# Two of seven normalised tiles transposed by VectorE blocks and on-chip DMAs instead of TensorE

## The chip, the cores and the metric

One core of a Trainium2 chip runs the whole kernel. The metric is the time on the device in microseconds, the median of a few runs; one execution is also recorded by the hardware profiler, and all rows below come from that one. PE is TensorE (PEld its weight loads), DVE is VectorE, ACT is ScalarE, POOL is GpSimd, and SP is the engine that issues the DMAs here.

## The reference: what is computed

Attention over 2 batches and 12 heads (448 positions, 64 dimensions each, scores capped by a tanh), whose output is laid out as 896 tokens of 768 values. Then two feed-forward blocks:

```
h = x @ w_in                                   # 896 x 1024
solu = h * softmax(h)
ln = (solu - mean) / sqrt(var + 1e-6) * g_ln   # per token
x2 = ln @ w_out                                # 896 x 768
out = (silu(x2 @ w_gate) * (x2 @ w_val)) @ w_out2
```

All numbers stay near float32: each operand is kept as a rounded part `hi` and a remainder `lo`, and a product is three matmuls (hi·hi, hi·lo, lo·hi).

## The kernel before, in words

The change lies in the first feed-forward block. The 896 tokens are seven tiles of 128 (t = 0 to 6). For each tile, `ff1_h(t)` computes h on PE in six steps of six matmuls of 512 columns into two PSUM banks, and its `tail` does the softmax and the norm: DVE takes the two maxima (TENSOR_REDUCE) and negates them, ACT takes the exponentials of both halves, DVE sums, takes the reciprocal, multiplies (two SCALAR_TENSOR_TENSOR) and gathers the variance (BN_STATS, BN_AGGR), POOL takes the power -1/2, and DVE (ACT from tile 4 on) applies scale and shift to 128x1024 values in the tile `ee`. Tiles 5 and 6 take their variance by squares on ACT. The small numbers live in `sms`.

`ff1_T(t)` then transposes the normed tile for the next product. PE does eight transposes of 128x128 in two PSUM banks `lt` (two runs of four), ACT copies each bank to the hi part (`hi_act`), DVE subtracts to get the lo part (`lo_dve`). Tiles 0 to 2 land in `lA` (384 columns), tiles 3 to 6 in `lB` (512).

`load_w_out(j)` brings a block of 128 columns of w_out in two halves (i = 0, 1; contraction chunks 0 to 3 and 4 to 7), in the order j = 0, 3, 1, 4, 2, 5. Each half goes through SP's load into one of two raw buffers, one ACT pass (`wo<-wo_raw`; two for j = 4, 2, 5), up to four DVE passes that end with the fill of the low bits from the raw buffer, four ACT passes of 128 columns that multiply by g_ln (`wo<-wo,gt`), the hi copy on ACT (`wo<-wo`, output rounded) and the lo subtraction on DVE. The blocks use three buffers of the pool `wo`. `ff1_x2(j, ...)` is the product of such a block with `lA` or `lB`; it is cut after the fourth chunk, so the second half of a product needs the second half of the block.

What PE does is a fixed list, each step written out in `run` (T[t] are the transposes of tile t, wo[i] the i-th block's loading, x2[i] its products):

```
steps = h[1] + h[2][:1] + T[0] + h[2][1:] + h[3][:1] + T[1] + h[3][1:] + wo[0] + h[4][:2] + T[2] + ...
steps = x2[0][0] + x2[0][1] + wo[2] + x2[1][0][:1] + T5 + x2[1][0][1:] + x2[1][1] + T6
steps += wo[3] + x2[2][0][:1] + x2[0][2] + x2[1][2] + ...
```

PE keeps this order; for DVE, ACT and SP a scheduler sets the order when the program is built (an instruction recorded while `in_order` is true keeps its place in the program). On the chip each engine works through its fixed queue in order, and an instruction whose operand is late holds all behind it on that engine. All calls go through one helper, so most rows carry line L54, and one goes by the tile names.

Of the kernel before, what the change touches and what calls it, by code (L numbers as in the profile page):

```python
# [5 lines left out]
F32 = mybir.dt.float32  # L6
# [55 lines left out]
class Kernel:  # L62
# [507 lines left out]
    def ff1_T(self, t, get, o):  # L570

        nc = self.nc

        def go(g):
            def f():
                l = get()
                ps = self.pt.tile([128, 512], F32, name=f"lt_{t}_{g}", tag=self.ttag)
                for i in range(4):
                    fc = 4 * g + i
                    self.transpose(ps[:, i * 128:(i + 1) * 128], self.ln[t][:, fc * 128:(fc + 1) * 128], self.ident)  # L580
                pv = ps.rearrange("p (i n) -> p i n", i=4)
                hi, lo = (l[:, 4 * g:4 * g + 4, u, o:o + 128] for u in range(2))
                self.hi_act(hi, pv)
                self.lo_dve(lo, pv, hi)
            return f

        return [(0.45, go(g)) for g in range(self.K1 // 4)]

    def load_w_out(self, j):

        w = self.wos[j] = self.wo.tile([128, 2, self.K1, 128], F32R, name=f"wo_{j}", tag="wo")
        for i in range(2):
            c = slice(4 * i, 4 * i + 4)
            src = self.w_out[i * 512:(i + 1) * 512, j * 128:(j + 1) * 128].rearrange("(f p) d -> p f d", p=128)
            if j in (4, 2, 5):
                f = self.f32_shifted(self.load_shifted(src, f"wo_{j}_{i}"), f"wo_{j}_{i}")
            else:
                f = self.f32(self.load64(src, f"wo_{j}_{i}"), f"wo_{j}_{i}", pin=True)
            f = f.rearrange("p (f d) -> p f d", f=4)
            for m in range(4):  # L600
                self.A.activation(f[:, m], f[:, m], AF.Copy, scale=self.gt[:, 4 * i + m:4 * i + m + 1])
            self.hi_act(w[:, 0, c], f)
            self.lo_dve(w[:, 1, c], f, w[:, 0, c])
# [92 lines left out]
    def x_hi(self, i):  # L696

        self.hi_act(self.T[i][:, 0], self.xf[i])

    def x_lo(self, i):  # L700

        self.lo_dve(self.T[i][:, 1], self.xf[i], self.T[i][:, 0])

# [138 lines left out]
    def seven_products(self, fc):  # L842
# [11 lines left out]
        X = lambda kh, th: [[self.x2[3 * kh + c][:, u, 448 * th:448 * th + 448] for u in range(2)] for c in range(3)]  # L854
        T1, T2, T3, T4 = ([[t[:, u, c] for u in range(2)] for c in range(3)] for t in self.T)

# [78 lines left out]
    def split(self, d, src):  # L935

        self.hi_act(d[0], src)
        self.lo_dve(d[1], src, d[0])
# [226 lines left out]
    def run(self):  # L1165
        nc = self.nc
        KD, K1, K2, F1 = self.KD, self.K1, self.K2, self.F1
# [17 lines left out]
        f, g, hi, lo = zip(*w)  # L1185
        self.w_steps = [((), f[0][:1], ()), (f[0][1:2], (), f[0][2:] + g[0][:1]), ((), (g[0][1], hi[0]), (lo[0],))]
        for i in range(1, KD):
            a = g[i][:1]
# [9 lines left out]
        h = [self.ff1_h(t) for t in range(7)]  # L1198
# [9 lines left out]
        st = self.pool("st", side="right")  # L1208
# [5 lines left out]
        self.pt = self.ph = self.pool("pm", bufs=8, space=PSUM)  # L1214
        self.htag, self.ttag = "m", "m"
        lA = self.slot("l", [128, K1, 2, 384], "lA")
        T = [self.ff1_T(t, lambda: lA, 128 * t) for t in range(3)]
        lp = self.pool("lp", side="right")
        self.wo = self.pool("wo", bufs=3, side="right")
        lB = lp.tile([128, K1, 2, 512], F32R, name="lB", tag="lB")  # L1220
        T3, T4 = self.ff1_T(3, lambda: lB, 0), self.ff1_T(4, lambda: lB, 128)
        T5, T6 = self.ff1_T(5, lambda: lB, 256), self.ff1_T(6, lambda: lB, 384)
        J = (0, 3, 1, 4, 2, 5)
        wo = [[(0.0, lambda j=j: self.load_w_out(j))] for j in J]
# [2 lines left out]
        whole = (blocks[0], (lambda: lB, 512, 384))  # L1227
        x2 = [[self.ff1_x2(j, *b) for b in (blocks if i < 2 else whole)] for i, j in enumerate(J)]

        steps = h[1] + h[2][:1] + T[0] + h[2][1:] + h[3][:1] + T[1] + h[3][1:] + wo[0] + h[4][:2] + T[2] + h[4][2:] + wo[1] + h[5][:5] + T3 + h[5][5:] + h[6][:-1] + T4 + h[6][-1:]  # L1230
        for _, f in steps:
            f()
        wp.release()
        n = self.HN = self.DM // 2
# [9 lines left out]
        steps = x2[0][0] + x2[0][1] + wo[2] + x2[1][0][:1] + T5 + x2[1][0][1:] + x2[1][1] + T6  # L1244
        steps += wo[3] + x2[2][0][:1] + x2[0][2] + x2[1][2] + [(0.0, lambda j=j: self.x_sums0(j)) for j in J[:2]]
        for j in range(2, KD):
# [4 lines left out]
            a, b = x2[j]  # L1251
# [10 lines left out]
        a12 = ap.tile([128, KD * 2 * 896], F32R, name="a_1", tag="a_1")  # L1262
        self.T = [a12[:, 2688 * i:2688 * i + 2688].rearrange("p (u k n) -> p u k n", u=2, k=3) for i in range(4)]
        self.A12t, self.A22t = (a12[:, KD * 2 * a:KD * 2 * z].rearrange("p (k u n) -> p k u n", k=KD, u=2)
# [89 lines left out]
```

## Time and profile before

| | |
|---|---|
| median of 3 runs | 471.57 us (470.81 to 471.76) |
| profiled execution, its own time | 471.51 us |
| its span, first to last instruction | 469.8 us |
| PE busy | 465.2 us, 99% of the span |
| DVE busy, ACT busy | 382.4 us (81%), 315.3 us (67%) |
| SP's DMA queue | 65936 packets, 51.84 MB |

The share of PE says that the time is the length of PE's list plus whatever PE has to wait; 1.7 us lie outside of the span. The first feed-forward block takes from about 108 to 228 us.

### The profile page before, as it was taken

Reading aid. Unit: us, or ns where it says so; the run is one execution under the profiler, and the core shown is the slowest. Engines: PE = TensorE matmul, PEld = TensorE weight load, DVE = VectorE, ACT = ScalarE, POOL = GpSimd, SP = SyncE. Lnnn points to the kernel's source line nnn. Section 1 sums busy time; section 2 is a strip of 40 time slices with the busy share of each in tenths; the row PEclk is TensorE's granted clock in tenths of the full one; section 3 lists DMA queues with packets and bytes.
Section 4 is the critical chain, followed back from the end, with each engine's and each line's share of the span. In section 5 each row is a group of like instructions: output and inputs, shape, how many; then the busy total and the mean of one; then the engine's idle time right before and its main releaser. Section 6 shows DMA issues by size and latency. Waiting matters only on the chain.

```text
span 469.8 us, 7726 instructions
## 1 busy us (share of the span) xinstructions
PE 465.2 (99%) x2970; PEld 385.1 (82%) x2970; DVE 382.4 (81%) x671; ACT 315.3 (67%) x480; POOL 37.2 (8%) x76
## 2 busy tenths in 40 slices
PE   9999999999999999999999999999999999999997
PEld 8444444446888899998989999999998889999996
DVE  3689999987777997766698989988897777999961
ACT  4999999961223699889676667766589988525200
POOL 1011010112000000000003211011000000000000
PEclk9999999999999999999999999999999999999999
DMA  7985575002000233535215523323447774010021
GB/s 179 215 201 117 165 190 165 21 1 77 14 1 0 78 102 116 175 114 178 91 46 184 173 87 130 120 76 124 136 134 221 249 207 130 26 43 18 0 85 67
DMA packets 66004, 52.33 MB, mean 111 GB/s; under 512 B 35760, under 2 KB 62128, under 8 KB 65200
## 3 DMA queue, kind: packets, MB, share of 16 engines
q1 hardware_dynamic: 65936, 51.84, 37.4%
q8 instruction: 23, 0.38, 0.3%
q14 instruction: 13, 0.11, 0.1%
q0 software_dynamic: 32, 0.00, 0.0%
HBM read 49.08 MB, written 2.75 MB: 110 GB/s over the span
## 4 chain that ended last, share of the span: by engine, by line
PE 99%; DVE 1%; issue 0%
PE p L54 17%; PE x L54 13%; PE g L54 12%; PE h L54 12%; PE pv L54 8%; PE sc L54 7%; PE b L54 6%; PE v L54 6%; PE c L54 6%; PE S L54 4%; PE e L54 3%; PE lt L54 1%; PE T L54 1%; PE warm L54 1%; DVE ks L54 0%; PE d L54 0%
## 5 line engine op out<-in xcount | busy, mean ns | idle before, releaser
L54 PE MATMUL g<-x,g 128*128 128x448 f32 (+2 forms) x288 | 62.2, 364 | 0.0
L54 PE MATMUL h<-wi,x 128*128 128x512 f32 x252 | 59.1, 392 | 0.0
L54 PEld LDWEIGHTS g<-x,g 128*128 128x128 f32 x288 | 53.2, 188 | 5.2
L54 PEld LDWEIGHTS h<-wi,x 128*128 128x128 f32 x252 | 46.8, 188 | 11.2 <-issue 1.5
L54 ACT ACTIVATE P<-sc,consts 112x896 f32<-112x896 f32 x48 | 45.4, 1010 | 3.8 <-PE sc L54 2.2
L54 ACT ACTIVATE P<-P,consts 112x3584 f32<-112x3584 f32 (+1 forms) x13 | 39.7, 3061 | 0.1
L54 PE MATMUL pv<-P,v 112*32 112x448 f32 x384 | 38.5, 540 | 0.0
L54 PEld LDWEIGHTS sc<-ks 64*112 64x112 f32 x288 | 23.3, 171 | 18.3 <-issue 8.4
L54 PE MATMUL sc<-ks 64*112 64x448 f32 x288 | 35.9, 379 | 0.2
L54 PE MATMUL x<-lB,wo 128*128 128x256 f32 (+1 forms) x192 | 35.2, 337 | 0.0
L54 PEld LDWEIGHTS x<-lB,wo 128*128 128x128 f32 x192 | 29.6, 189 | 3.4
L54 PE MATMUL b<-a,g 128*128 128x448 f32 x144 | 31.8, 365 | 0.0
L54 ACT ACTIVATE ee<-h,sms 128x512 f32<-128x512 f32 x14 | 9.5, 684 | 33.2 <-DVE sms L54 33.2
L54 PEld LDWEIGHTS pv<-P,v 112*32 112x32 f32 x384 | 12.2, 110 | 23.0 <-issue 20.9
L54 PE MATMUL v<-x,g 128*128 128x384 f32 (+1 forms) x144 | 30.1, 362 | 0.0
L54 PEld LDWEIGHTS b<-a,g 128*128 128x128 f32 x144 | 27.1, 188 | 2.1
L54 PEld LDWEIGHTS v<-x,g 128*128 128x128 f32 x144 | 26.1, 188 | 2.8
L54 PE MATMUL x<-lA,wo 128*128 128x384 f32 x144 | 27.2, 338 | 0.0
L54 PEld LDWEIGHTS x<-lA,wo 128*128 128x128 f32 x144 | 25.2, 188 | 0.5
L54 PE MATMUL S<-P,ones 112*32 112x448 f32 x192 | 22.4, 549 | 0.0
L54 POOL COPY sm<-tr 32x14 f32<-32x14 f32 x48 | 15.0, 312 | 93.0 <-DVE tr L54 91.5
L54 DVE TENSOR_TENSOR x<-x,x 128x448 fp32r<-128x448 f32 (+3 forms) x26 | 15.3, 588 | 8.3 <-ACT x L54 7.6
(277 smaller groups left out, 970.4 us busy)
## 6 DMA issues: line engine op xcount, KB each, us to landing
wg_raw<-in_moe_w_gate_dram SPq DMA_DIRECT2D x11, 765.8 KB, 4.2
wv_raw<-in_moe_w_val_dram SPq DMA_DIRECT2D x10, 765.8 KB, 4.3
h<-in_moe_w_out_dram SPq DMA_DIRECT2D x18, 383.6 KB, 3.6
wi_raw<-in_moe_w_in_dram SPq DMA_DIRECT2D x6, 1024.0 KB, 6.3
wo_raw<-in_moe_w_out_dram SPq DMA_DIRECT2D x6, 512.0 KB, 3.5
wo_raw<-in_moe_w_out_dram SPq DMA_DIRECT2D x6, 510.5 KB, 3.7
v<-in_v_dram SPq DMA_DIRECT2D x24, 112.0 KB, 3.4
kq<-in_k_dram SPq DMA_DIRECT2D x22, 112.0 KB, 3.1
```

The costliest lines, as they stand in the source:

```text
L54: i = f(*a, **k)
```

## The change

For tiles 0 and 1, the PE transposes with their PSUM banks, four ACT copies and four DVE subtractions go. In their place `moved` takes a buffer of the pool `wo`, transposes the normed tile on DVE in blocks of 32x32 (one STREAM_TRANSPOSE of 128x1024 into the first half `y`), and puts the blocks where a full transpose has them by 16 DMAs per tile (`y` to `z`, each 32 partitions by 8 by 32 values). `split` then makes hi and lo of all 128x1024 values at once, in program order behind the next tile's tail.

```
+    def ff1_T_moved(self, t, get, o):
+        st, K1 = {}, self.K1
+        def moved():
+            b = self.wo.tile([128, 2 * self.F1], F32, name=f"lt_{t}", tag="wo")
+            y, z = b[:, :self.F1], b[:, self.F1:].rearrange("p (f n) -> p f n", f=K1)
+            st["z"] = z
+            self.V.transpose(y, self.ln[t])
+            for g in range(4):
+                for a in range(4):
+                    src = y[32 * a:32 * a + 32].rearrange("p (f g n) -> p g f n", f=K1, g=4)[:, g]
+                    self.nc.sync.dma_start(z[32 * g:32 * g + 32, :, 32 * a:32 * a + 32], src)
+        def split():
+            hi, lo = (get()[:, :, u, o:o + 128] for u in range(2))
+            was, self.in_order = self.in_order, True
+            self.split((hi, lo), st["z"])
+            self.in_order = was
+        return [(0.0, moved)], [(0.0, split)]
...
-        T = [self.ff1_T(t, lambda: lA, 128 * t) for t in range(3)]
...
+        (T0, s0), (T1, s1) = (self.ff1_T_moved(t, lambda: lA, 128 * t) for t in range(2))
+        T2 = self.ff1_T(2, lambda: lA, 256)
...
-        steps = h[1] + h[2][:1] + T[0] + h[2][1:] + h[3][:1] + T[1] + h[3][1:] + wo[0] + h[4][:2] + T[2] + h[4][2:] + wo[1] + h[5][:5] + T3 + h[5][5:] + h[6][:-1] + T4 + h[6][-1:]
+        steps = h[1] + h[2][:1] + T0 + h[2][1:] + s0 + h[3][:1] + T1 + h[3][1:] + s1 + wo[0] + h[4][:2] + T2 + h[4][2:] + wo[1] + h[5][:5] + T3 + h[5][5:] + h[6][:-1] + T4 + h[6][-1:]
```

PE's list is otherwise the same, row for row. The scheduler's orders for DVE, ACT and SP differ from there to the end of the block. Three places:

ACT where tile 5 is transposed, before. `lt_5_0` and `lt_5_1` are the two banks of tile 5's transposes, `wo_3_1` is the second half of the block j = 3, `wo_3` its finished block, `wo_1_0` the first half of block j = 1, `ee<-ee,sms` the norm of tile 6:

```order
L54 ACTIVATE wo_3_1756<-wo_3_1_1773 128x512
L54 ACTIVATE h_6_0_1853,sms_168<-ee_169,sms_168 128x512
L54 ACTIVATE h_6_1_1854,sms_168<-ee_169,sms_168 128x512
L54 ACTIVATE lB_1468<-lt_5_0_2031 128x4x128
L54 ACTIVATE lB_1468<-lt_5_1_2038 128x4x128
L54 ACTIVATE wo_1_0_1992<-wo_1_0_1992,gt_113 128x128 x4
```

The same place with the change:

```order
L54 ACTIVATE h_6_1_1866,sms_168<-ee_169,sms_168 128x512
L54 ACTIVATE x2_1946<-x2_0_384_1974 128x256
L54 ACTIVATE wo_1_0_2004<-wo_1_0_raw_2002 128x512
L54 ACTIVATE lB_1468<-lt_5_0_2043 128x4x128
L54 ACTIVATE wo_3_1_1785<-wo_3_1_1785,gt_113 128x128 x4
L54 ACTIVATE lB_1468<-lt_5_1_2050 128x4x128
L54 ACTIVATE ee_169<-ee_169,sms_168 128x1024
L54 ACTIVATE wo_3_1768<-wo_3_1_1785 128x512
L54 ACTIVATE wo_1_0_2004<-wo_1_0_2004,gt_113 128x128 x4
L54 ACTIVATE wo_1_2001<-wo_1_0_2004 128x512
```

The hi copy of the second half of block 3 stood ahead of the two copies of tile 5's transposes; it now stands behind both of them, behind its own four scalings and behind tile 6's norm.

DVE from tile 2's variance to its norm, before (`h_3` is the next tile's product; the one TENSOR_SCALAR right behind BN_AGGR adds 1e-6 and starts POOL, the next one takes POOL's result):

```order
L54 BN_AGGR sms_168<-sms_168 128x2
L54 TENSOR_SCALAR sms_168<-sms_168 128x1
L54 TENSOR_REDUCE sms_168<-h_3_0_1591 128x1
L54 TENSOR_SCALAR sms_168<-sms_168 128x1
L54 TENSOR_REDUCE sms_168<-h_3_1_1592 128x1
L54 TENSOR_SCALAR ee_169<-ee_169,sms_168 128x1024
```

With the change:

```order
L54 BN_AGGR sms_168<-sms_168 128x2
L54 TENSOR_REDUCE sms_168<-h_3_0_1597 128x1
L54 TENSOR_SCALAR sms_168<-sms_168 128x1
L54 TENSOR_REDUCE sms_168<-h_3_1_1598 128x1
L54 TENSOR_SCALAR sms_168<-sms_168 128x1 x2
L54 TENSOR_SCALAR ee_169<-ee_169,sms_168 128x1024
L54 TENSOR_TENSOR lA_1461<-lt_0_1531,lA_1461 128x8x128
```

The addition that starts POOL went behind the first reduce, and the lo part of tile 0 now stands behind the norm.

DVE around the lo part of the second half of block 0 (`wo_0` from `wo_0_1`), before:

```order
L54 SCALAR_TENSOR_TENSOR ee_169,sms_168<-ee_169,sms_168,h_5_1_1786 128x512
L54 TENSOR_TENSOR wo_0_1659<-wo_0_1_1676,wo_0_1659 128x512
L54 TENSOR_REDUCE sms_168<-h_6_0_1853 128x1
L54 TENSOR_REDUCE sms_168<-h_6_1_1854 128x1
```

With the change:

```order
L54 TENSOR_REDUCE sms_168<-h_6_0_1865 128x1
L54 TENSOR_SCALAR wo_3_0_1771<-wo_3_0_1771 128x512
L54 TENSOR_REDUCE sms_168<-h_6_1_1866 128x1
L54 SCALAR_TENSOR_TENSOR wo_3_0_1771<-wo_3_0_raw_1769,wo_3_0_1771 128x512
L54 TENSOR_SCALAR sms_168<-sms_168 128x1 x2
L54 SCALAR_TENSOR_TENSOR wo_3_0_1771<-wo_3_0_raw_1769,wo_3_0_1771 128x512
L54 TENSOR_TENSOR wo_0_1671<-wo_0_1_1688,wo_0_1671 128x512
```

The subtraction stood ahead of the reduces of tile 6's product; it now stands behind them and behind three passes of block 3.

## Rows read from the trace of the kernel before

**Rows 1.** The page, part 1 and part 2: engine, busy us; forty slices in tenths.

```profile
PE 465.2 (99%) x2970; PEld 385.1 (82%) x2970; DVE 382.4 (81%) x671; ACT 315.3 (67%) x480; POOL 37.2 (8%) x76
...
PEclk9999999999999999999999999999999999999999
```

**Rows 2.** Timeline of PE, 120 to 194 us: start, length, engine, operation, tiles, count.

```profile
123.44 1.04 PE L54 MATMUL lt<-ident,ee 128*128 128x128 f32 x8
124.23 8.42 PE L54 MATMUL h<-wi,x 128*128 128x512 f32 x36
132.60 1.09 PE L54 MATMUL lt<-ident,ee 128*128 128x128 f32 x8
133.45 9.80 PE L54 MATMUL h<-wi,x 128*128 128x512 f32 x42
143.09 1.04 PE L54 MATMUL lt<-ident,ee 128*128 128x128 f32 x8
...
166.64 1.03 PE L54 MATMUL lt<-ident,ee 128*128 128x128 f32 x8
167.43 4.43 PE L54 MATMUL x<-lA,wo 128*128 128x384 f32 x24
...
176.66 1.03 PE L54 MATMUL lt<-ident,ee 128*128 128x128 f32 x8
177.45 2.33 PE L54 MATMUL x<-lA,wo 128*128 128x384 f32 x12
...
183.28 2.35 PE L54 MATMUL x<-lA,wo 128*128 128x384 f32 x12
185.47 8.66 PE L54 MATMUL x<-lB,wo 128*128 128x256 f32 x60
```

**Rows 3.** Groups of DVE instructions by form: busy us, mean ns of one.

```profile
L54 DVE STREAM_TRANSPOSE tr<-sm 128x448 f32<-128x448 f32 x12 | 7.7, 645 | 0.4
...
L54 DVE TENSOR_TENSOR wi<-wi,wi 128x1024 fp32r<-128x1024 f32 x6 | 7.3, 1225 | 0.2
```

**Rows 4.** Timeline of DVE, 131 to 142 us, idle time and its end in brackets.

```profile
138.94 0.21 DVE L54 BATCH_NORM_AGGREGATE sms<-sms 128x2 f32<-128x12 f32 x1
...
140.34 0.69 DVE L54 TENSOR_REDUCE sms<-h 128x1 f32<-128x512 f32 x1 [1.00 <-PE h L54]
...
141.66 0.81 DVE L54 TENSOR_SCALAR ee<-ee,sms 128x1024 f32<-128x1024 f32 x1
```

**Rows 5.** Timeline of DVE, 163 to 170 us.

```profile
163.34 0.69 DVE L54 SCALAR_TENSOR_TENSOR wo<-wo_raw,wo 128x512 uint32<-128x512 uint32 x1
...
166.21 0.69 DVE L54 TENSOR_TENSOR wo<-wo,wo 128x512 fp32r<-128x512 f32 x1
166.81 1.28 DVE L54 TENSOR_REDUCE sms<-h 128x1 f32<-128x512 f32 x2
```

**Rows 6.** Timeline of ACT, 167 to 185 us.

```profile
167.28 0.60 ACT L54 ACTIVATE lB<-lt 128x512 fp32r<-128x512 f32 x1 [0.55 <-PE lt L54]
...
177.55 1.07 ACT L54 ACTIVATE lB<-lt 128x512 fp32r<-128x512 f32 x2
178.60 1.28 ACT L54 ACTIVATE wo<-wo,gt 128x128 f32<-128x128 f32 x4
...
180.20 1.23 ACT L54 ACTIVATE ee<-ee,sms 128x1024 f32<-128x1024 f32 x1
181.34 0.62 ACT L54 ACTIVATE wo<-wo 128x512 fp32r<-128x512 f32 x1
...
184.09 0.77 ACT L54 ACTIVATE wo<-wo_raw,consts 128x512 f32<-128x512 int8 x1
```

**Rows 7.** DMA of SP: issues, then totals of 20 to 90 us.

```profile
73.14 1.28 SPq L280 DMA_DIRECT2D kq<-in_k_dram  x2
...
q1 hardware_dynamic: 24059, 11.00, 61.1%
...
kq<-in_k_dram SPq DMA_DIRECT2D x15, 112.0 KB, 3.1
```

## The prediction

> **What bounds the kernel now.** The page first: PE is busy in 99% of the span, DVE in 81% and ACT in 67% [rows 1]. So only two things can move the time: fewer products in PE's list, or a place where PE waits. The clock is granted in full in all slices [rows 1] (2.4 of the two levels 1.2 and 2.4 GHz). PE's timeline next: around the transposes each run starts where the one before it stops, with no idle time in brackets [rows 2]. The timelines of DVE and ACT show why: what PE needs is ready shortly before PE gets there. Tile 2's norm ends at 142.47, the transposes that read it start at 143.09 [rows 2, 4]. The hi part of the second half of w_out's block 3 is followed by tile 5's copies at 177.55, and the product that needs it starts at 177.45 [rows 2, 6]. So a small gap in PE's favour is all there is, and the order of the rows on ACT and DVE decides.
>
> **What is removed.** Two runs of eight transposes: 124.23 - 123.44 = 0.79 us and 133.45 - 132.60 = 0.85 us [rows 2], together **-1.64 us** of PE. That is the whole gain; ACT and DVE are off the path, what they lose or gain counts only where PE waits. With them go four ACT copies and four DVE subtractions; added are two ACT copies and two subtractions of twice to 2.3 times that size.
>
> **What is added.** DVE's block transpose of 128x1024 is not in the trace; one of 128x448 takes 0.645 us [rows 3]. Below: no less than that, 0.65. Above: in proportion, 1.47. A subtraction takes 0.69 for 512 elements [rows 5] and 1.225 for 1024 [rows 3], so 0.00104 per element and a fixed part of 0.16; by the same step of 576 elements the transpose takes 0.645 + 0.60 = 1.24, which I take, since the kinds are near each other. The subtraction of a whole tile is priced at that 1.225. The 32 DMAs: SP issues one of 448 pieces in 0.64 us (1.28 for two), and one lands 3.1 us after issue [rows 7]. Sixteen then take 16 x 0.64 + 3.1 = 13.4 us. The first tile's last block lands at about 124.0 + 13.4 = 137.4, the second's at 134.5 + 13.4 = 147.9. ACT's place for these copies is behind tile 2's exponentials (136.1) and behind tile 2's own copies (143.6), DVE's place for the last subtraction is at 150.4, so both are in time, by 1.3 us in the second case. SP's next row, block 3's load, waits for a raw buffer until about 154 and so loses nothing. Price of the DMAs on the path: nothing, up to that 1.3 us.
>
> **What moves: four places where PE now waits.** I took the new order of each engine row by row, with each row beginning when the row before it and its inputs are done, and with the durations of the rows of before. The same walk through the old order ends the block within 0.2 us of the trace.
>
> *Tile 2's norm.* Ahead of its BN_AGGR, DVE gets two block transposes (+2.5) and loses three subtractions of 0.6 on its path, and the exponentials come 0.3 earlier as copies leave ACT: 138.94 becomes 139.3 [rows 4]. The product h_3 is done 1.64 earlier (140.34, for which DVE idled 1.00, becomes 138.7 [rows 4]). DVE is now the late one. And the addition that starts POOL stands behind the first reduce: 0.6 reduce, 0.15 addition, 0.7 POOL, 0.25 for two small rows, so the norm starts at about 141.15 and ends at 141.95. A weight load needs some 0.2 more; PE is there at 143.09 - 1.64 = 141.45. **+0.7**; with a block transpose of 0.65 it is nothing, with one of 1.47 it is 1.1.
>
> *The lo part of block 0's second half.* It stood ahead of tile 6's reduces, at 166.21 [rows 5], for a product that starts twelve matmuls behind 167.43 [rows 2]. Now it stands behind two reduces (1.28), two fills of block 3 (0.6 each from the next start [rows 5], like the subtraction itself), a shift (0.4), two small rows (0.3) and its own 0.7: 3.8 us from the end of h_6's first bank. PE needs 0.79 (tile 4's transposes), 2.19 (twelve products, 183.28 to 185.47) and two more products (0.36) less 0.2 for the weight load: 3.1. **+0.7**, between 0 and 1.
>
> *The hi part of block 3's second half.* This is the large one. ACT's row for tile 5's first bank waits for PE's transposes: 0.64 us after they start (166.64 to 167.28 [rows 2, 6]). Behind it, in the new order: that copy 0.5, the four scalings 1.24, the second bank's copy 0.5, tile 6's norm 1.14, the hi copy 0.62 (each to the next start, last one to its end [rows 6]): 4.0. So the hi part is there 4.6 us after tile 5's transposes begin, and PE, which has only those transposes to do in between, wants it after 0.79 (176.66 to 177.45), with its weight load 0.2 before: **+4.05**. It hardly depends on anything else, since the chain starts at PE's own transposes: however early PE comes, it waits as long. The lo part follows 0.7 later, the third product wants it 0.35 later: **+0.35**.
>
> *Tile 6's lo part.* The first product of lB's second pair of tiles starts 8.02 after block 3's second half (177.45 to 185.47 [rows 2]), 8.4 with the 0.35. On ACT stand three groups of scalings, hi copy, raw pass, two passes of block 4 (0.77 and 0.7), two copies of finished products and the tile's own copy, 7.5 in sum, and some 1.5 of waits for block 4's load and fill, then 0.7 of DVE: **+1.25**; without those waits nothing.
>
> Later steps: DVE, ACT and the loads get more time by each wait of PE, and PE's list and their orders are the same from there on. No more is added.
>
> **Sum.** -1.64 + 0.7 + 0.7 + 4.05 + 0.35 + 1.25 = +5.4 us on the profiled execution's 471.51 (its span of 469.8 and 1.7 around it), which stands 0.06 under the median: **476.9 us**, 1.1% slower, chance 0.55, in a range of its own of 475.6 to 478.2. A difference of under 0.2% (0.94 us) could not be told from none.
>
> **Rivals.**
>
> *Only the long wait.* The other three waits are differences of 0.7 to 1.25 us between long chains, and PE's own lateness takes them away if DVE or ACT run a little ahead of my walk. For it: the block before shows such gaps of 0.2 to 0.6 and no wait. Against it: all three sit behind rows that stood elsewhere. -1.64 + 4.05 = +2.4: 473.9. Chance 0.17.
>
> *The blocks land late.* If a block DMA of 128-byte pieces costs more than the rows show, ACT stands at tile 1's copy with block 0 and tile 4's exponentials behind it. 24059 packets took 61.1% of 70 us on 16 engines, 28 ns each [rows 7]; 4096 of them on all sixteen are 7.3 us a tile, on half of them 14.6, and then the last lands 17.7 us after the transpose instead of 13.4. It decides from 14.7 on: 3 us later at ACT and DVE, of which PE, through tile 4's norm and block 0, waits about 2.1. 479.0. Chance 0.11. The Trainium skill bears on this in two places of "DMA: Bandwidth & Descriptors": its Specifications put transfers under 512 B below line rate, its section "Why small descriptors are slow (HBM only)" exempts transfers between SBUF and SBUF. By the first this rival gains, by the second the blocks are in time; no row of before has an on-chip transfer, so I lean on neither.
>
> *The clock falls in the long wait.* All rows have PE at work and the clock at 2.4 GHz, so none shows what four idle microseconds do. If the clock went to 1.2 GHz for about as long as the wait, 4 us of products would take twice as long for half of their work: 2 us lost, of which up to 1.25 come back as the wait for tile 6 goes. +0.75 to +2: 477.7 to 478.9. Chance 0.12. The Trainium skill, "TensorE: Matmul & The Clock Gate", section "Why this matters for your kernels", says that an idle gap between matmul bursts drops the engine to half rate and asks to keep gaps short; by that rule this rival is what happens, and no run here has shown it.
>
> *No wait that matters (the other side).* PE loses its sixteen transposes and everything arrives in time: 469.9, 0.35% faster. It needs the long wait gone: ACT would have to do the five rows behind tile 5's first bank within 0.3 us instead of 4.0, or PE to come 4 us late to tile 5 for another reason. It decides where the waits together fall under 1.64. For it speaks that the old order had no waits at all, against it that the rows stand in this order in the program. Chance 0.04. The last 0.01 is that the change does nothing that can be seen.
>
> **Range and chances.** 473.9 (only the long wait) to 479.2 (late blocks, or the clock at its dearest). Slower by over 0.2%: 0.94, within 0.2%: 0.02, faster: 0.04.
>
> **What would show it.** In the changed kernel's PE timeline, an idle time of about 4 us behind tile 5's transposes, ended by ACT `wo`; smaller ones before tile 2's transposes (ended by DVE `ee`), in the first product with block 0 (DVE `wo`) and before the first product of lB's second pair of tiles (DVE `lB`). The granted clock stays full. The block transposes are about 1.24 us long, the DMAs land before ACT asks for them, and nothing on ACT waits for them. PE's total is 1.6 us less. I am wrong if PE shows no wait at tile 5, if ACT idles for a DMA at `lA`, or if the clock falls; or if a later stage, which I take as unmoved, shows a wait that was not there.

## The result and the profile after

The changed kernel takes 476.46 us (median of 4 executions, 475.68 to 476.57), the kernel before 471.55: a ratio of 1.0103, 95% interval 1.0086 to 1.0121. It is 4.9 us slower. The profiled execution took 476.57 us with a span of 474.8, so 5.0 more than the span of before.

The page of the changed kernel, parts 1 and 2:

```profile
PE 466.0 (98%) x2954; PEld 385.4 (81%) x2954; DVE 384.1 (81%) x671; ACT 315.5 (66%) x478; POOL 37.8 (8%) x76
...
PEclk9999999999999997999999999999999999999999
```

Beside [rows 1], PE has 16 instructions fewer, yet is busy for 0.8 us more: some of its work went slower. The one slice with a 7 says where. The waits of PE (line, releaser; us in total, times, longest):

```profile
PE x L54 <- ACT wo L54: 3.5, 1, 3.5
...
PE lt L54 <- DVE ee L54: 0.5, 1, 0.5
PE x L54 <- DVE wo L54: 0.2, 1, 0.2
```

None of these three is in the trace of before. PE's timeline of the changed kernel, to be laid beside [rows 2]:

```profile
141.07 1.09 PE L54 MATMUL lt<-ident,ee 128*128 128x128 f32 x8 [0.50 <-DVE ee L54]
...
165.49 2.70 PE L54 MATMUL x<-lA,wo 128*128 128x384 f32 x14
168.39 2.01 PE L54 MATMUL x<-lA,wo 128*128 128x384 f32 x10 [0.20 <-DVE wo L54]
...
175.19 1.03 PE L54 MATMUL lt<-ident,ee 128*128 128x128 f32 x8
179.77 4.29 PE L54 MATMUL x<-lA,wo 128*128 128x384 f32 x12 [3.54 <-ACT wo L54]
183.86 3.83 PE L54 MATMUL x<-lB,wo 128*128 128x256 f32 x24
187.53 1.04 PE L54 MATMUL lt<-ident,ee 128*128 128x128 f32 x8
...
199.00 2.27 PE L54 MATMUL x<-lA,wo 128*128 128x384 f32 x12
```

Two rows of before that [rows 2] leaves out stand at the same places:

```profile
182.48 1.04 PE L54 MATMUL lt<-ident,ee 128*128 128x128 f32 x8
...
193.96 2.27 PE L54 MATMUL x<-lA,wo 128*128 128x384 f32 x12
```

The twelve products at 179.77 take 4.29 us where they took 2.33 [rows 2], and the 24 behind them take 3.83. Half-microsecond stretches of the same trace (busy time of PE with instructions, granted clock, DMA share, GB/s) show the reason:

```profile
178.00:178.50 0.50, 0.00 (x0) 1.00 0.65 227
178.50:179.00 0.50, 0.00 (x0) 0.79 0.01 2
179.00:179.50 0.50, 0.00 (x0) 0.50 0.00 0
...
185.00:185.50 0.50, 0.50 (x4) 0.50 0.00 0
185.50:186.00 0.50, 0.50 (x6) 0.88 0.00 0
```

From about 178.8, some 2.6 us after PE fell idle, to about 185.6 the granted clock is 0.50 of full, so 1.2 GHz. The same set of work can now be measured place by place, from the start of one set of PE's rows to the next, before against after:

- up to the first unbroken run of `h` products: 108.30 against 107.59, -0.71. Nothing of the change stands there. The first 18 `sc` products start at 7.59 before and at 6.94 after; in the other profiled runs of this study they start between 6.47 and 7.82, at 6.77 and 7.82 in two kernels without a moved tile. It is the spread of the start.
- from there to tile 2's transposes: 34.79 against 33.48, -1.31 (16 transposes gone, a wait of 0.50; without that wait it is 1.81 less, 0.17 more than the 1.64 of the transposes).
- to tile 5's transposes: 33.57 against 34.12, +0.55 (the wait of 0.20, and slower starts round it).
- tile 5's transposes and the wait behind them: 0.79 against 4.58, +3.79.
- the 36 products behind the wait: 5.03 against 7.76, +2.73.
- from tile 6's transposes to the end of the span: 287.3 in both.

The sum is +5.0. ACT at the place of the long wait, changed kernel:

```profile
175.82 0.60 ACT L54 ACTIVATE lB<-lt 128x512 fp32r<-128x512 f32 x1 [1.32 <-PE lt L54]
176.32 1.26 ACT L54 ACTIVATE wo<-wo,gt 128x128 f32<-128x128 f32 x4
177.49 0.57 ACT L54 ACTIVATE lB<-lt 128x512 fp32r<-128x512 f32 x1
177.97 1.23 ACT L54 ACTIVATE ee<-ee,sms 128x1024 f32<-128x1024 f32 x1
179.10 0.62 ACT L54 ACTIVATE wo<-wo 128x512 fp32r<-128x512 f32 x1
```

ACT itself idles 1.32 us for PE's transposes, and then PE idles through five rows of ACT. Each engine waits for the other in turn, which no total of busy time shows. In [rows 6] the two copies of tile 5 stand next to each other at 177.55, and the hi copy is done ahead of them, 1.2 us before the product that needs it starts (177.45):

```profile
175.61 0.62 ACT L54 ACTIVATE wo<-wo 128x512 fp32r<-128x512 f32 x1
```

Last, the new operations, from the groups by form (mean ns of one; idle before), first DVE's, then ACT's, and the DMA part of 120 to 152 us:

```profile
L54 DVE STREAM_TRANSPOSE lt<-ee 128x1024 f32<-128x1024 f32 x2 | 2.5, 1239 | 0.0
L54 DVE TENSOR_TENSOR lA<-lt,lA 128x1024 fp32r<-128x1024 f32 x2 | 2.4, 1218 | 0.0
```

```profile
L54 ACT ACTIVATE lA<-lt 128x1024 fp32r<-128x1024 f32 x2 | 2.1, 1062 | 5.1 <-DMA lt<-lt 5.1
```

```profile
q1 hardware_dynamic: 8704, 1.05, 20.3%
...
lt<-lt SPq DMA_DIRECT2D x32, 32.0 KB, 1.9
```

ACT stood 5.1 us for the blocks, 4.1 of it at tile 1. Whether PE pays for that is the first question of the experiments.

### The profile page after: what moved, and what is told of

Its sections match the earlier page's. It is cut to its first block, busy times and chain, and to the rows that moved or that the text cites. A ratio compares the mean times of both kernels' runs of the same rounds, so it can differ in the third digit from the quotient of the medians.

```text
span 474.8 us, 7731 instructions
## 1 busy us (share of the span) xinstructions
PE 466.0 (98%) x2954; PEld 385.4 (81%) x2954; DVE 384.1 (81%) x671; ACT 315.5 (66%) x478; POOL 37.8 (8%) x76
## 4 chain that ended last, share of the span: by engine, by line
PE 91%; DVE 4%; SPq 2%; ACT 1%; issue 0%; POOL 0%; DMA 0%; POOLq 0%
PE p L54 16%; PE x L54 13%; PE g L54 12%; PE pv L54 8%; PE sc L54 7%; PE h L54 6%; PE b L54 6%; PE v L54 6%; PE c L54 6%; PE S L54 4%; PE e L54 3%; SPq L602 2%; DVE sms L54 2%; DVE ee L54 1%; PE T L54 1%; PE warm L54 1%
## 5 line engine op out<-in xcount | busy, mean ns | idle before, releaser
L54 PEld LDWEIGHTS x<-lB,wo 128*128 128x128 f32 x192 | 30.6, 196 | 3.4
L54 PE MATMUL x<-lA,wo 128*128 128x384 f32 x144 | 29.5, 356 | 3.7 <-ACT wo L54 3.5
L54 PEld LDWEIGHTS x<-lA,wo 128*128 128x128 f32 x144 | 26.7, 199 | 5.1 <-ACT wo L54 3.8
```

Source lines behind the costliest of these rows:

```text
L54: i = f(*a, **k)
```

## The experiments

The theory: the list of steps and the moved tiles gave the scheduler another order, in which the hi copy of block 3's second half stands on ACT behind tile 5's first bank; PE waits for it, and its clock falls with the wait. The rivals: the on-chip transfers cost the time; the extra work on DVE costs it; a moved tile costs time wherever it stands. A ratio is always to runs of the kernel before on the same chip.

**Without the transfers.** The block transposes write straight into the half that the splits read:

```diff
-            self.V.transpose(y, self.ln[t])
-            for g in range(4):
-                for a in range(4):
...
+            self.V.transpose(b[:, self.F1:], self.ln[t])
```

> Leaves out the 32 on-chip transfers: the block transposes write straight to where the splits read, so the blocks stand in wrong places and the output is not the reference's. Every row on ACT behind tile 5's first bank stands as in the changed kernel. If the order of ACT's rows makes the wait (my theory): the same 3.5 us wait of PE behind tile 5, ended by ACT wo, the same fall of the clock behind it, and 476.4 (475.7 to 477.0); ACT's idle 1.0 and 4.1 us before lA, which a DMA ended, go, and PE sees nothing of it. If the transfers are what costs (rival): ACT and DVE run up to 4 us earlier from tile 1's split on, the waits of PE shrink with them, and the time is 471 to 474.

Measured: 475.97 us, ratio 1.0100 (1.0086 to 1.0114). PE's waits:

```profile
PE x L54 <- ACT wo L54: 3.5, 1, 3.5
...
PE lt L54 <- DVE ee L54: 0.5, 1, 0.5
PE x L54 <- DVE wo L54: 0.2, 1, 0.2
```

They are those of the changed kernel one by one, with no on-chip transfer in this block. ACT no longer idles for blocks. The 32 transfers and ACT's 5.1 us of waiting for them cost nothing that PE sees; the 0.5 us less than in the changed kernel is less than what the clock alone differed between the two traces (7.76 against 6.60 us for the 36 products behind the wait). In the changed kernel the chain that ended last does run through SP's issues:

```profile
PE 91%; DVE 4%; SPq 2%; ACT 1%; issue 0%; POOL 0%; DMA 0%; POOLq 0%
```

That 2% is an inference about who released whom; taking the work away shows that it held up nothing.

**The order alone.** In the kernel before, with no tile moved, `wo[1]` (the load and the fixing of block 3) is put out directly behind `wo[0]`:

```diff
-... + T[1] + h[3][1:] + wo[0] + h[4][:2] + T[2] + h[4][2:] + wo[1] + h[5][:5] + T3 + ...
+... + T[1] + h[3][1:] + wo[0] + wo[1] + h[4][:2] + T[2] + h[4][2:] + h[5][:5] + T3 + ...
```

> The kernel before, no tile moved; only wo[1] is put out directly behind wo[0], ahead of h_4 and tile 2, which sends block 3's second-half scalings and hi copy behind tile 5's first bank on ACT. If ACT's order makes the wait (my theory): PE waits about 4 us behind tile 5's transposes for ACT wo, the clock falls to half behind it, and the time is 478.5 (476.0 to 480.5). If it takes the moved tiles to make the wait (rival): 471.5 (470.8 to 472.5).

Measured: 476.76 us, ratio 1.0121 (1.0104 to 1.0139), in the range expected, 1.7 us under the 478.5. PE's timeline and then ACT's:

```profile
180.35 3.68 PE L54 MATMUL x<-lA,wo 128*128 128x384 f32 x12 [3.54 <-ACT wo L54]
...
187.33 1.04 PE L54 MATMUL lt<-ident,ee 128*128 128x128 f32 x8
```

```profile
176.41 0.60 ACT L54 ACTIVATE lB<-lt 128x512 fp32r<-128x512 f32 x1 [0.69 <-PE lt L54]
176.90 1.26 ACT L54 ACTIVATE wo<-wo,gt 128x128 f32<-128x128 f32 x4
178.07 0.58 ACT L54 ACTIVATE lB<-lt 128x512 fp32r<-128x512 f32 x1
178.55 1.23 ACT L54 ACTIVATE ee<-ee,sms 128x1024 f32<-128x1024 f32 x1
179.68 0.62 ACT L54 ACTIVATE wo<-wo 128x512 fp32r<-128x512 f32 x1
```

The same five rows and the same 3.54 us, without a moved tile. The clock falls here too, but not during the wait: it is full until about 181.8, 1.5 us after the products have started again, and then at half for 3.4 us:

```profile
181.50:182.00 0.50, 0.50 (x5) 0.84 0.83 176
```

The order is enough. Neither this edit nor the next ones move a single row: the scheduler sets other rows differently with each. What ties the loss to these five rows is that in all six kernels that have them (three more come below) the products with block 3's second half start 4.57 or 4.58 us after tile 5's transposes do, and in no other kernel later than 1.8 us after.

**The order put back, tiles moved.** In the changed kernel tile 2's steps go behind three of `h_4`'s steps:

```diff
-... + wo[0] + h[4][:2] + T2 + h[4][2:] + wo[1] + ...
+... + wo[0] + h[4][:3] + T2 + h[4][3:] + wo[1] + ...
```

> The changed kernel with one edit: tile 2's steps stand behind three of h_4's steps instead of two. The two moved tiles, their 32 transfers and the large splits all stay; on ACT the hi copy of block 3's second half and its four scalings stand ahead of tile 5's first bank again, as in the kernel before. If the order is the cause (my theory): no wait over 0.6 us behind tile 5, full clock, 16 transposes less on PE: 470.2 (469.6 to 471.0), faster than the kernel before. If moved tiles cost time by themselves, by their transfers or the extra DVE work: 474 to 477, with waits of PE before tile 2 or in the products with lA.

Measured: 469.52 us, ratio 0.9959 (0.9944 to 0.9973): faster than the kernel before by 1.7 us, about the 1.64 of the transposes removed, and 0.1 us under the range expected. PE's timeline, then ACT's:

```profile
175.09 1.03 PE L54 MATMUL lt<-ident,ee 128*128 128x128 f32 x8
175.88 2.33 PE L54 MATMUL x<-lA,wo 128*128 128x384 f32 x12
```

```profile
174.31 0.62 ACT L54 ACTIVATE wo<-wo 128x512 fp32r<-128x512 f32 x1
175.73 0.60 ACT L54 ACTIVATE lB<-lt 128x512 fp32r<-128x512 f32 x1 [0.80 <-PE lt L54]
```

The hi copy (174.31) is again ahead of tile 5's first bank, and all three of PE's new waits are gone, with both tiles moved and ACT still waiting 4.3 us for blocks. (This trace has one wait of PE that the others have not, 0.41 us for a load at 18 us, far ahead of the change.)

**Its control.** The same edit in the kernel before (`h[4][:3] + T[2] + h[4][3:]`).

> The control for the order put back: the kernel before, no tile moved, with the same edit (tile 2's steps behind three of h_4's steps). If the gain of that run over the kernel before is that of the moved tiles' 16 transposes (my theory): this is the kernel before again, 471.2 (470.8 to 471.7), PE without a wait. If it was the edit of the order that gained (rival): 469.5 to 470.3.

Measured: 471.13 us, ratio 1.0000 (0.9992 to 1.0009), no new wait. So the 1.7 us are not the edit's; they are the moved tiles', once the order stands.

**One tile moved.** Tile 1 is transposed on PE again:

```diff
-        (T0, s0), (T1, s1) = (self.ff1_T_moved(t, lambda: lA, 128 * t) for t in range(2))
+        (T0, s0), (T1, s1) = self.ff1_T_moved(0, lambda: lA, 0), (self.ff1_T(1, lambda: lA, 128), [])
```

> Only tile 0 is moved, tile 1 is transposed on PE; the list of steps as in the changed kernel. On ACT the hi copy of block 3's second half stands ahead of tile 5's first bank, as in the kernel before. If the order of those rows makes the loss (my theory): no long wait, full clock, 8 transposes less: 470.5 (469.8 to 471.4). If each moved tile costs time: about half of the loss of two, 473 to 474.5.

Measured: 470.82 us, ratio 0.9995 (0.9985 to 1.0004). No long wait, as expected, and not half of the loss; but a gain that can't be told from none: eight transposes are gone, and tile 1's transposes now waited 0.43 us for their norm, which stands behind the block transpose on DVE. On ACT the hi copy of block 3 (175.05) stands ahead of tile 5's first bank (176.39).

**Only tile 1's split later.** Both tiles moved, `s1` behind tile 2's steps:

```diff
-... + h[3][:1] + T1 + h[3][1:] + s1 + wo[0] + h[4][:2] + T2 + h[4][2:] + ...
+... + h[3][:1] + T1 + h[3][1:] + wo[0] + h[4][:2] + T2 + s1 + h[4][2:] + ...
```

> Both tiles moved, tile 2 at its old place in h_4; only tile 1's split is put out behind tile 2's steps instead of ahead of block 0's. This too puts block 3's hi copy ahead of tile 5's first bank on ACT, but leaves two block transposes ahead of tile 2's norm. My theory: no long wait and full clock, tile 2's norm still late by 0.5 us: 470.2 (469.6 to 471.2). If the two block transposes on DVE make the loss (rival): 474 to 476, as in the changed kernel.

Measured: 470.37 us, ratio 0.9987 (0.9976 to 0.9997). Tile 2's norm is still 0.50 us late and a lo part 0.34; the long wait is gone. Two different edits that put the hi copy ahead of tile 5 both remove it. What is left of the price of the order on DVE in this run is these two waits, 0.84 us together. Why the scheduler put the hi copy behind tile 5 with two moved tiles, and ahead of it with one or with a later split, no run shows.

**A third tile moved**, on top of the order put back: tile 2 by `ff1_T_moved` as well, `wo[0]` behind it, its split `s2` put out among `h_4`'s last steps:

```diff
-        T2 = self.ff1_T(2, lambda: lA, 256)
+        T2, s2 = self.ff1_T_moved(2, lambda: lA, 256)
...
-... + s1 + wo[0] + h[4][:3] + T2 + h[4][3:] + wo[1] + ...
+... + s1 + h[4][:3] + T2 + wo[0] + h[4][3:-2] + s2 + h[4][-2:] + wo[1] + ...
```

> Tile 2 is moved as well (a third buffer of the same pool ahead of block 0's, 16 more transfers, its split put out among h_4's last steps), on top of the order put back; block 3's hi copy stands ahead of tile 5's first bank. Eight transposes less again: 468.7 (468.2 to 469.4) if every wait stays away; if its split is late for block 0's first product with lA, behind block 0's scalings and tile 5's norm on ACT, PE waits for it by 1 to 4 us and the clock may fall with it: 469.5 to 474.

Measured: 474.01 us, ratio 1.0065 (1.0052 to 1.0079). The second case of the expectation, at its upper end: the split comes too late. PE's timeline, then ACT's:

```profile
165.93 0.44 PE L54 MATMUL x<-lA,wo 128*128 128x384 f32 x1 [0.93 <-ACT lA L54]
167.54 4.26 PE L54 MATMUL x<-lA,wo 128*128 128x384 f32 x23 [1.17 <-DVE lA L54]
...
178.40 2.73 PE L54 MATMUL x<-lA,wo 128*128 128x384 f32 x12 [0.77 <-ACT wo L54]
```

```profile
161.44 1.27 ACT L54 ACTIVATE wo<-wo,gt 128x128 f32<-128x128 f32 x4
...
164.84 1.04 ACT L54 ACTIVATE lA<-lt 128x1024 fp32r<-128x1024 f32 x1
```

The blocks are there (the copy at 164.84 has no wait), but it stands behind block 0's scalings, and between them tile 4's norm (the expectation calls it tile 5's), block 3's raw pass and block 0's hi copy, one straight after the other. Again ACT's order, not the transfer. The 0.77 us behind tile 5's transposes are for block 3's hi copy, which here stands ahead of tile 5's banks but behind tile 6's norm. The profiled execution kept its clock; the three others had mean granted clocks of 0.996 and took 473.85 to 474.40, so no longer for it.

**What the clock costs.** Small products into a spare bank behind tile 5's transposes keep PE busy in the long wait; 24 of them first (48 in the trace, where each shows as two):

```diff
-        steps = x2[0][0] + x2[0][1] + wo[2] + x2[1][0][:1] + T5 + x2[1][0][1:] + x2[1][1] + T6
+        steps = x2[0][0] + x2[0][1] + wo[2] + x2[1][0][:1] + T5 + [(0.0, lambda: self.keep_warm(24, self.pt.tile([128, 512], F32, name="warm_T5", tag="m")))] + x2[1][0][1:] + x2[1][1] + T6
```

> Adds 24 products of 64x64 into a spare bank behind tile 5's transposes, so that PE works in most of the long wait; order of ACT and DVE as in the changed kernel. If the clock fell because PE idled (my theory): the granted clock stays full, the products with block 3's second half take 5.0 instead of 7.8 us, some of which the wait for tile 6's lo part takes back (up to 1.1), and the time is 474.8 (473.8 to 475.4); block 3's second half still comes as late as before, about 4.6 us after tile 5's transposes begin. If the clock falls for another reason, such as the kind of products there: 476.5 and the clock at half again.

Measured: 475.22 us, ratio 1.0078 (1.0062 to 1.0094), granted clock full in its trace:

```profile
175.74 3.01 PE L54 MATMUL warm_T<-const-float32-1.0 128*64 128x64 f32 x48
179.35 2.75 PE L54 MATMUL x<-lA,wo 128*128 128x384 f32 x12 [0.60 <-ACT wo L54]
...
184.81 1.04 PE L54 MATMUL lt<-ident,ee 128*128 128x128 f32 x8
```

The 36 products take 5.46 us instead of 7.76, so the slow clock cost 2.30 there, and the 0.43 over the 5.03 of before is block 3's lo part, for which PE's weight loads wait 0.43 us (ended by DVE `wo`). The run has two blemishes: the scheduler counted the small products and turned two rows of ACT round at tile 6, against what was expected of it, and PE waited 1.0 us at 262 for a later block. So the same with 18, which leaves ACT's and DVE's order as it is:

> As the run with 24 small products, but with 18, few enough that the order of ACT's and DVE's rows is that of the changed kernel row for row (with 24 the scheduler also turned two rows round at tile 6). The clock should stay full. If tile 6's lo part is late by itself, as I forecast (+1.25), and only the slow products hid it in the changed kernel: block 3's second half takes 5.5 us up to tile 6's transposes instead of 7.8, and PE then waits 1.1 to 1.5 us for DVE lB before lB's second pair of tiles; 475.5 (475.0 to 476.1), so the clock's own price is only 0.9. If tile 6's lo part is in time (rival, my term was wrong): no wait there and 474.2 (473.7 to 474.8).

PE's timeline:

```profile
179.69 2.75 PE L54 MATMUL x<-lA,wo 128*128 128x384 f32 x12 [1.30 <-ACT wo L54]
...
185.15 1.03 PE L54 MATMUL lt<-ident,ee 128*128 128x128 f32 x8
...
188.50 0.39 PE L54 MATMUL x<-lB,wo 128*128 128x256 f32 x1 [0.21 <-ACT lB L54]
189.23 8.63 PE L54 MATMUL x<-lB,wo 128*128 128x256 f32 x59 [0.34 <-DVE lB L54]
197.70 2.27 PE L54 MATMUL x<-lA,wo 128*128 128x384 f32 x12
```

With the clock full, tile 6 is late: from its transposes to the next set with `lA` PE needs 12.55 us, against 11.47 in the changed kernel and 11.48 before. From the end of the long wait to that set it is 18.01 against 19.23 in the changed kernel. So between these two traces 1.08 of the clock's 2.30 us would have been waited for anyway, and 1.22 are its own. That is no fixed price: in the run without transfers, whose rows on ACT are the same there, the clock was at half for 3.4 us instead of 6.8, and the same stretch (180.54 to 198.62) took 18.08 us, only 0.07 more than the 18.01. The time itself was missed: the profiled execution took 475.24, inside the 475.0 to 476.1, but the five spread from there to 477.73 (median 476.85, ratio 1.0125, 1.0107 to 1.0143), all with a granted clock of 0.999 or more. What the others waited for is not in any trace that was taken, and the median shows no gain from the full clock over the changed kernel's 1.0103.

With 8 of them, 1.15 us of work and 2.47 of idle time behind it:

> The same with 8 small products, about 1 us of work and so some 2.5 us of idle time left behind tile 5, rows of ACT and DVE in the changed kernel's order. Waits of up to 1.2 us have left the clock alone so far, the one of 3.5 us brought it down in three kernels. If 2.5 us is enough: clock at half for 3 to 7 us behind the wait and no wait at tile 6, 476.2 (475.7 to 476.6). If it isn't: full clock, the wait at tile 6 of 1.1 to 1.5 us, 475.5 (475.0 to 476.0).

Measured: 475.83 us (474.96 to 476.13), ratio 1.0100 (1.0086 to 1.0114). It went both ways: the profiled execution, the fastest, kept its clock and shows the wait of 0.34 for DVE `lB`; the three others had mean granted clocks of 0.996 and took 475.58 to 476.13, so 0.6 to 1.2 us more in one and the same kernel. That is a comparison of four executions, one of them with a trace.

## Why the prediction was right

The forecast of 476.9 stands against 476.46, within its own range, and the mechanism is the one named: the order of rows on ACT at tile 5. Term by term:

- **Transposes, -1.64.** Held: with the order put back, the moved tiles gain 1.6 to 1.7 us (469.52 against 471.21 for the kernel before and 471.13 for it with the same edit).
- **Cost of the added work.** The block transpose takes 1.239 us (forecast 1.24), the subtraction 1.218 (1.225). ACT begins the second tile's copy at 146.96, 13.2 us after the transpose ended at 133.77, against the 13.4 for the last block. That "nothing on ACT waits for them" failed: ACT idled 1.0 and 4.1 us, which the prediction had named as a sign against itself. Its own figures said so: blocks at 137.4 and 147.9 against places on ACT at 136.1 and 143.6 are 1.3 and 4.3 us of standing, and "in time" held only for DVE's place at 150.4. PE paid nothing for it, as the run without transfers shows. The rival of late blocks did not come true: the last block was there no later than forecast, and a packet took 12 ns of an engine, not 28.
- **Tile 2's norm, +0.7.** The wait is 0.50, in place and releaser as forecast.
- **Lo part of block 0, +0.7.** A wait of 0.20, in all 0.55 longer in that stretch.
- **Hi part of block 3, +4.05, lo +0.35.** 3.79 and 0.43. The long wait is most of the loss, and both the run with the order alone and those with the order put back show that the order of ACT's rows causes it.
- **Tile 6's lo part, +1.25.** Not there in the changed kernel, and yet real: 1.08 with the clock full. In the changed kernel the slow products hid it.
- **The clock.** The prediction said that it stays full, with 0.12 for the rival. That step was wrong: it fell in all four executions (means of 0.993 to 0.996), for a gross 2.30 us. The rival's working, twice the time for half of 4 us less what comes back at tile 6, gave +0.75 to +2; the changed kernel's trace gives +1.22, the one without transfers +0.07. The rule of the Trainium skill that stood beside it ("TensorE: Matmul & The Clock Gate", section "Why this matters for your kernels": an idle gap between matmul bursts drops the engine to half rate) agrees with the changed kernel's trace, where the clock fell 2.6 us into the wait, and it should have had more weight than the rows of before, in which PE never idles.

So the total came out close partly by luck, because errors offset each other. The waits were forecast at 7.05 in sum and are 0.50 + 0.55 + 3.79 + 0.43 + 1.08 = 6.35, so 0.70 too much; the clock's own 1.22 was left out; and the profiled execution gained 0.71 at its start, which is spread and no effect of the change. With the 0.17 beyond the transposes, -1.64 - 0.17 + 6.35 + 1.22 - 0.71 = +5.05, the 5.0 between the two spans.

## What to carry to other kernels

In this kernel, with one engine busy for 99% of the span, taking work off it gained only where the rows of the other engines kept their order. Look at what the scheduler did to the rows around each hand-over, above all where engine A waits for B and B for A in turn, before counting the gain. Here the fix was to move one group of steps by one place, and the change of 1% slower became 0.4% faster. The long wait of TensorE cost more than its length, by 0.07 to 1.22 us of slow clock in two traces, and the slow products hid 1.08 us of lateness that stood behind it: neither is to be added without the other.

## What was not expected of the hardware

- The clock at 1.2 GHz: in the changed kernel it fell 2.6 us into a wait of 3.5 and stayed for 6.8 us; in the run without transfers it fell 3.4 us into the same wait and stayed for 3.4; in the run with the order alone it fell 1.5 us after that wait had ended, with PE at work again, and stayed for 3.4. The 36 products behind the wait then took 7.76 and 6.60 us, and 6.98 in the run with the order alone, all behind the same 3.54 us of idle time. A wait of 2.47 us left it full in the profiled run with 8 small products, and waits of 0.9 and 1.2 us in the profiled run with three tiles; in both kernels the three other executions had means of 0.996, so the expectation's "Waits of up to 1.2 us have left the clock alone so far" held for the trace alone.
- On-chip transfers of 128-byte pieces were cheaper by the packet than the loads, and dearer by the byte: 8704 packets in 32 us took 20.3% of 16 engines, 12 ns each, against 28 ns in [rows 7], but a packet there carries 457 bytes on average and here 120, so a kilobyte took some 99 ns of an engine against 62. One transfer of 32 KB lands in 1.9 us, one of 112 KB there in 3.1. The Trainium skill ("DMA: Bandwidth & Descriptors", section "Why small descriptors are slow (HBM only)") exempts transfers between SBUF and SBUF from the price of small pieces; this trace agrees with that by the packet and not by the byte. What made the blocks late is that SP issued them one after the other, 32 in 22.2 us.
